# Two more products of the up projection in two levels, and the attention's last transposes divided

## The chip, the cores and the metric

The kernel runs on one core of one Trainium2 chip. The metric is the device time of the program in microseconds (us). A core has TensorE (PE, matrix products; its weight loads are listed as PEld), VectorE (DVE), ScalarE (ACT), GpSimd (POOL, here used to issue DMAs) and SyncE (SP, which issues DMAs too). PE reads SBUF and writes PSUM, whose banks are shared out by tags in this kernel.

## The reference

A lightning attention block over 4 batches, 8 heads, 768 tokens and head dimension 64, then a two-layer block on the 3072 x 512 result:

```python
for b in range(nb):                      # blocks of 64 tokens
    intra = np.einsum('bhic,bhjc->bhij', qb, kb) * Dmask[None]
    intra = np.einsum('bhij,bhjd->bhid', intra, vb)
    inter = np.einsum('bhid,bhde->bhie', qb * lam_pow[None], kv_state)
    out[:, :, sl] = intra + inter
    kv_state = lam_block[None, :, None, None] * kv_state + np.einsum('bhsd,bhse->bhde', kb_dec, vb)
x = attn_out.transpose(0, 2, 1, 3).reshape(B * S, H * D)     # 3072 x 512
h = x @ w_in                                                 # 512 -> 2048, "up"
g = h - np.tanh(h)
out = g @ w_out                                              # 2048 -> 512, "down"
```

All in float32.

## The kernel before, in words

**Groups.** Tokens are worked on in six groups of 512 (`NG = 6`, g = 0 to 5): 128 tokens of each of the four batches, a batch's part being a chunk. While group g goes through up and down, the attention of group g + 1 is done in between. The code from group 2 on (`GI = 2`) differs from that of the first two groups; the change concerns mostly groups 2 to 5.

**Products by seven.** Both projections use Strassen's scheme in Winograd's form: a 2 x 2 block product with seven products of blocks, P1 to P7, of sums of blocks, instead of eight. `FACT` names the two factors of each. In up, the four result blocks of the hidden layer are called 11, 12, 21 and 22, held as g11, g12, g21, g22 with a fifth tile, gS ("S1"); each is 128 x (4 u x 512): u counts four parts of the hidden dimension. The blocks come out as

- 11: P1 + P2
- 12: P1 + P6 + P5 + P3
- 21: P1 + P6 + P7 + P4
- 22: P1 + P6 + P7 + P5

**One or two levels.** An ordinary product of up for one u (`up(g, u, n)`) is four matmuls of 128x256, so sixteen for the four u. "In two levels" a product is itself done by the seven-product scheme, in seven steps of four matmuls of 128x128 (`STEPS = (1, 2, 6, 5, 7, 3, 4)`). For up that is `inner_steps`: before, for P1, P2 and P5 (`INNER`) of groups 2 to 5. Its weights for steps 5, 6, 3 are sums of weight quarters, made once by `inner_weights` in group 1, written to DRAM (`fine_in`) and read back a piece at a time; its token sums are made by `inner_tokens`. After the steps the results are put together by three DVE adds and four ACT copies of 128x512. For down, `down_twice` does the same, with hidden sums made by `sums_twice`; inside it, at its second step, DVE forms a12 - s2 (L817), which a later step (3) reads.

**Seeds.** A product that adds to a sum held in SBUF starts from a PSUM bank into which ACT has copied that sum (`seed`). Before, in groups 2 to 5, P6 is added to P1 in PSUM (bank "y" seeded with g12 by `seed_up`), copied back to g12 (L570), P7 and then P4 go on in the same bank, and P3 in a bank "z" seeded with P5 (g22). `finish` takes tanh (ACT, L561) and subtracts (DVE, L562).

**Order.** The last loop of the kernel, over g, writes out the order. Around the change, in groups 2 to 5: for each u the products P3, P7, P6 (of u + 2), P4, with the seven steps of down's P1 (`p_first`) spread among them; then down's P2, the first half of the attention's output of g + 1 (`att_out(g + 1, (0, 1))`), down's P4, P5, P6, the second half, P7; then P3 of down interleaved with P1 and P2 of up of the next group, then P5 of up and the first two P6. DVE also transposes the queries and keys of group g + 1 (`att_transpose`, L362 and L373, one chunk at a time) and decays its keys (`att_decay`, L399): chunks 0 and 1 in the loop over u, chunks 2 and 3 by `run(p1[0:1])` between down's P4 and P5. The weights of down and of `inner_steps` come through a ring of seven buffers (`RING`, `piece`, `send`) whose reads POOL issues in the order of `stream`, as buffers come free.

Instructions are put in their engine's queue by a scheduler that follows the written order unless something further down is ready sooner by its own estimate. `tied` (`keep_in_program_order`) pins an instruction behind the one written before it on the same engine.

Of the kernel before, what the change touches and what calls it, by code (L numbers as in the profile page):

```python
# [24 lines left out]
def kernel(  # L25
# [188 lines left out]
    TWICE = (3, 5, 6, 4, 7, 1, 2)  # L214
    fine = dram.tile([len(TWICE), len(SUB), 128, NU, 128], F32, name="fine")

    fine_in = dram.tile([3, 3, 128, NU, 128], F32, name="fine_in")
    w_in_u = moe_w_in.rearrange("k (a n) -> k a n", a=2)
    blocks = [("in", u, i) for u in range(NU) for i in range(KI)] + [("out", kt, a) for kt in range(KH)
                                                                    for a in range(2)]  # L220
# [180 lines left out]
    def kv_products(g, bs):  # L401

        kv = bank("kv", *(("yb", 1) if g >= GB else ("att", 4))).rearrange("d (b p e) -> d b p e", b=2, p=NP)
        for n, b in enumerate(bs):
            kd, vn = raw[g, b]["k"], raw[g, b]["v"]
            for p in range(NP):
                for j in range(2):
                    tied(g == 0, nc.tensor.matmul(out=kv[ts(j, 64), n, p, :], lhsT=kd[:, 2 * p + j, :],  # L408
                                                  rhs=vn[:, 2 * p + j, :], start=n == 0 and p == 0, stop=True,
                                                  skip_group_check=True))  # L410
        return kv
# [10 lines left out]
    def att_read(g, bs):  # L422
        ops = [bank("op", *x).rearrange("d (p b s) -> d p b s", p=2, b=2)
               for x in ((("ya", 1), ("z", 1)) if g >= GB else (("att", 4),) * 2)]
        decayed = None
        if g > 0:
            st = state[:, bs[0]:bs[0] + 2]
            for n, b in enumerate(bs):
                for p in (0, 1):
                    for j in range(2):  # L430
                        r = ts(j, 64)
                        for pp in (p, p + 2):
                            nc.tensor.matmul(out=out_dst(ops, n, pp, j), lhsT=state[r, b, pp, :],  # L433
                                             rhs=tr[g, b][2][r, pp, :], start=n == 0 and p == 0, stop=False,
                                             skip_group_check=True)
# [90 lines left out]
    def seed(key, x, tag, src):  # L526

        banks[key, x] = bank(x, tag, 1)
        tied(x == "y" and key[2] < 2, nc.scalar.activation(banks[key, x].rearrange("q (m c) -> q m c", m=2), src, AF.Copy))

    def hidden(g, c):

# [2 lines left out]
        return hid[g, c]  # L535

    def seed_up(g, u):
        seed(("up", g, u), "y", ("yb", "w", "ya")[u % 3], hidden(g, 12)[:, u])

    def up(g, u, n):  # L540
        a, bname = FACT[n]
        wt = {"A11": w1[u][:, 0:2, 0], "A12": w1[u][:, 2:4, 0], "S3": w1[u][:, 0:2, 1], "A22": w1[u][:, 2:4, 1],
              "S1": ws[u][:, 0], "S2": ws[u][:, 1], "S4": ws[u][:, 2]}[a]
        x = xt[g][bname] if bname != "B11" else xt[g, 0][:, 0:2]
        key = ("up", g, u)
        if g >= GI and n == 6 and u > 1:
            seed_up(g, u)
        if g >= GI and n == 3:
            seed(key, "z", "z", hidden(g, 22)[:, u])
        t, first = product_bank(key, n)  # L550
        for m in range(2):
            for kt in range(2):
                nc.tensor.matmul(out=t[:, m, :], lhsT=wt[:, kt, ts(m, 128)], rhs=x[:, kt, :],  # L553
                                 start=first and m == 0 and kt == 0, stop=kt == 1, skip_group_check=True)

        def dst(c):
            return hidden(g, c)[:, u]

        def finish(c, src):
            th = work.tile([128, 2, HB], F32, name="th", tag="th")  # L560
            nc.scalar.activation(th, src, AF.Tanh)  # L561
            nc.vector.tensor_tensor(dst(c), src, th, op=AL.subtract)  # L562

        y, z, w = (banks[key, x].rearrange("q (m c) -> q m c", m=2) if (key, x) in banks else None for x in "yzw")
        if n == 1:
            seed(key, "w", "w", y)
        elif n == 2:
            finish(11, w)
        elif n == 6:
            nc.scalar.activation(dst(12), y, AF.Copy)  # L570
        elif n == 7:
            if g < GI:
                nc.scalar.activation(dst(22), y, AF.Copy)
            nc.vector.tensor_tensor(dst(22), dst(22), z if g < GI else y, op=AL.add)  # L574
            finish(22, dst(22))
        elif n == 4:
            finish(21, y)
        elif n == 3:
            nc.vector.tensor_tensor(dst(12), dst(12), z, op=AL.add)  # L579
            finish(12, dst(12))  # L580
        if n == (3 if g < GI else 7):
            nc.vector.tensor_tensor(dst("S1"), dst(12), dst(22), op=AL.add)
            nc.vector.tensor_tensor(dst(12), dst(11), dst(12), op=AL.subtract)

# [7 lines left out]

    INNER = (1, 2, 5)
    toks = {}

    def a_quarter(n, u, i, k):
        return (ws[u][:, 0, k] if n == 5 else w1[u][:, 2 * n - 2 + k, 0])[:, ts(i, 128)]

    def inner_weights(u, ns=INNER):
        for n in ns:
            a11, a12, a21, a22 = (a_quarter(n, u, i, k) for i in range(2) for k in range(2))
            t = late["pool"].tile([128, 4, 128], F32, name="ws2", tag="sums", bufs=6)
            s1, s2, s4 = (t[:, x] for x in range(3))
            for dst, x, y, op in ((s1, a21, a22, AL.add), (s2, s1, a11, AL.subtract), (a21, a11, a21, AL.subtract),
                                  (s4, a12, s2, AL.subtract)):
                tc.keep_in_program_order(nc.vector.tensor_tensor(dst, x, y, op=op))
            (nc.sync if u == NU - 1 else nc.gpsimd).dma_start(out=fine_in[INNER.index(n)].rearrange("x p u c -> p u x c")[:, u], in_=t[:, 0:3])

    def inner_tokens(g):
        for n in INNER:
# [9 lines left out]

    def inner_steps(g, n):

        tags = {1: ("yb", "att", "att"), 2: ("w", "att", "att"), 5: ("ya", "att", "z")}[n]
        y, w, z = (bank(x, tag, 4 if tag == "att" else 1) for x, tag in zip(("y3", "w3", "z3"), tags))
        r5 = otile("r5")
        out4 = hidden(g, {1: 12, 2: 11, 5: 22}[n])
        c11, c12, c21, c22 = (out4[:, :, i, ts(j, 128)] for i in range(2) for j in range(2))
        for x in STEPS:  # L630
            b = toks[g, n][x]
# [30 lines left out]
    def pieces_of(g):  # L662
# [5 lines left out]
        for x in STEPS:  # L668
            yield g, 3, x
            if x in (3, 5, 6):  # L670
                yield from ((g + 1, ("in", n), x) for n in (1, 2))
        yield from ((g + 1, ("in", 5), x) for x in STEPS if x in (3, 5, 6))

    stream = [x for g in range(1, NG) for x in pieces_of(g)]
    sent = {"n": 0}
# [168 lines left out]
    def every(steps):  # L844
        for _ in steps:
            pass
# [181 lines left out]
    for g in range(1, NG):  # L1028
        last = g == NG - 1
        p0, p1 = attention(g + 1) if not last else ([], [])  # L1030
        if g < GI:
            p_first = down(g, 1)
        else:
            sums_twice(g, 1)
            p_first = down_twice(g, 1)
        for u in range(NU):
            if g < GI:
                for n in (2, 6, 5, 7, 1, 4, 3):
# [10 lines left out]
                            fine_pieces(*p)  # L1049
            else:  # L1050
                up(g, u, 3)
                up(g, u, 7)
                if u + 2 < NU:
                    up(g, u + 2, 6)
                else:
                    next(p_first)
                up(g, u, 4)
                if u + 1 == NU:
                    sums_twice(g, 2)
                if u != 2:  # L1060
                    steps(p_first, (2, 1, 0, 2)[u])
                if not last and u < 2:
                    att_transpose(g + 1, (u,))
                elif not last:
# [27 lines left out]
        if g == GI - 1:  # L1092
            inner_weights(NU - 1, INNER[:2])
            steps(p4, 4)
            inner_weights(NU - 1, INNER[2:])
# [44 lines left out]

# [28 lines left out]
```

## Time and profile before

| What | Value |
|---|---|
| Time, median of 3 runs | 653.97 us (653.42 to 654.21) |
| The profiled execution's own time | 652.32 us |
| Its span on the core | 650.5 us |
| Mean granted TensorE clock | 1.000 |
| PE busy | 641.9 us, 99% of the span |
| DVE busy | 499.6 us, 77% |
| ACT busy | 250.4 us, 38% |
| POOL busy | 242.1 us, 37% |
| DMA | 135.79 MB, mean 209 GB/s |

A trace row gives start and length in us, the engine, the line, the operation, the tile written and those read, the shape, the number of instructions merged into the row, and in brackets the engine's idle time before it with what ended it. Lengths include the pipeline's latency, so the distance from one start to the next is what an instruction occupies. Times are from the span's start.

### The profile page before, as it was taken

How to read it: one execution, taken by the hardware profiler on the slowest of the kernel's cores; microseconds unless marked ns; L12 is line 12 of the kernel's file. 1: busy time of each engine (PE TensorE's matmuls, PEld its weight loads, DVE VectorE, ACT ScalarE, POOL GpSimd, SP SyncE). 2: the span in 40 equal slices, each digit the busy share in tenths (PEclk: the TensorE clock that was granted, in tenths of full speed). 3: DMA queues.
4: the chain of work that ended last, by engine and by line, in shares of the span. 5: the costliest groups of instructions: out<-in, count | busy, mean ns of one | idle time of the engine just before them, and what ended most of it. 6: DMA issues, size and time to landing. Idle time of an engine off the chain costs nothing. (4 is left out here: it accounts for less than half of the span.)

```text
span 650.5 us, 15718 instructions
## 1 busy us (share of the span) xinstructions
PE 641.9 (99%) x6080; PEld 595.6 (92%) x6080; DVE 499.6 (77%) x969; ACT 250.4 (38%) x513; POOL 242.1 (37%) x418
## 2 busy tenths in 40 slices
PE   8999999999999999999999999999999999999998
PEld 7888888888888999999999989999998999998997
DVE  4467889968999895778986678998477997485873
ACT  3686765523222222533222453213453313264210
POOL 6000136767756335203335302443411354411341
PEclk9999999999999999999999999999999999999999
DMA  9869987988979758958757967766967686612474
GB/s 200 213 170 192 251 257 226 383 250 232 270 195 269 240 190 259 209 125 219 241 166 229 249 132 170 223 234 208 232 137 157 206 265 213 235 69 66 158 246 163
DMA packets 160281, 135.79 MB, mean 209 GB/s; under 512 B 128640, under 2 KB 130944, under 8 KB 160208
## 3 DMA queue, kind: packets, MB, share of 16 engines
q0 software_dynamic: 30496, 97.88, 47.0%
q1 hardware_dynamic: 128096, 36.53, 26.7%
q8 instruction: 48, 0.79, 0.5%
q10 hardware_dynamic: 1616, 0.39, 0.4%
q14 instruction: 25, 0.20, 0.1%
HBM read 110.10 MB, written 24.64 MB: 207 GB/s over the span
## 5 line engine op out<-in xcount | busy, mean ns | idle before, releaser
L696 POOL DMA_DIRECT2D wb<-fine x204 | 110.0, 540 | 245.7 <-PE y L811 159.6
L815 ACT ACTIVATE q<-y 128x128 f32<-128x128 f32 x112 | 31.0, 277 | 144.6 <-PE y L811 143.6
L811 PE MATMUL y<-wb,g 128*128 128x128 f32 x584 | 76.6, 277 | 0.0
L811 PEld LDWEIGHTS y<-wb,g 128*128 128x128 f32 x584 | 70.7, 192 | 0.7
L870 PE MATMUL h<-xt,w 128*128 128x256 f32 x256 | 57.8, 383 | 0.4 <-DVE w L325 0.4
L870 PEld LDWEIGHTS h<-xt,w 128*128 128x128 f32 x256 | 47.6, 190 | 7.9 <-DVE w L325 1.3
L811 PE MATMUL zw<-wb,g 128*128 128x128 f32 x368 | 48.7, 276 | 0.0
L561 ACT ACTIVATE th<-g 128x512 f32<-128x512 f32 x40 | 25.2, 630 | 60.0 <-DVE g L579 42.2
L562 DVE TENSOR_TENSOR g<-g,th 128x512 f32<-128x512 f32 x40 | 27.7, 691 | 24.5 <-ACT th L561 24.4
L811 PEld LDWEIGHTS zw<-wb,g 128*128 128x128 f32 x368 | 44.8, 192 | 0.2 <-DVE g L817 0.2
L553 PE MATMUL y<-xt,w 128*128 128x256 f32 x192 | 45.0, 380 | 0.0
L553 PEld LDWEIGHTS y<-xt,w 128*128 128x128 f32 x192 | 36.5, 190 | 5.0 <-ACT g L570 0.2
L553 PE MATMUL z<-xt,ws 128*128 128x256 f32 x160 | 38.8, 381 | 0.1
L553 PE MATMUL y<-tt,w 128*128 128x256 f32 x160 | 38.3, 382 | 0.0
L811 PE MATMUL zw<-wb,s 128*128 128x128 f32 x280 | 37.9, 276 | 0.0
L553 PE MATMUL y<-tt,ws 128*128 128x256 f32 x160 | 37.8, 380 | 0.0
L811 PE MATMUL y<-wb,s 128*128 128x128 f32 x280 | 37.5, 277 | 0.0
L811 PEld LDWEIGHTS zw<-wb,s 128*128 128x128 f32 x280 | 35.2, 192 | 0.4
L811 PEld LDWEIGHTS y<-wb,s 128*128 128x128 f32 x280 | 34.7, 192 | 0.7
L553 PEld LDWEIGHTS y<-tt,w 128*128 128x128 f32 x160 | 29.9, 190 | 4.7 <-DVE g L574 0.5
L900 PE MATMUL acc<-wt,g 128*128 128x256 f32 x144 | 33.5, 382 | 0.4 <-DVE g L906 0.2
L553 PEld LDWEIGHTS y<-tt,ws 128*128 128x128 f32 x160 | 29.9, 191 | 3.6
(215 smaller groups left out, 1448.8 us busy)
## 6 DMA issues: line engine op xcount, KB each, us to landing
wb<-fine POOLq DMA_DIRECT2D x204, 256.0 KB, 3.7
wb<-fine_in POOLq DMA_DIRECT2D x36, 256.0 KB, 4.3
raw<-in_moe_w_out_dram SPq DMA_DIRECT2D x12, 512.0 KB, 5.6
rest<-fine POOLq DMA_DIRECT2D x20, 256.0 KB, 4.5
raw<-in_moe_w_in_dram SPq DMA_DIRECT2D x16, 256.0 KB, 6.4
fine<-f POOLq DMA_DIRECT2D x16, 256.0 KB, 4.6
q_blk<-in_q_dram SPq DMA_DIRECT2D x128, 32.0 KB, 3.3
k_blk<-in_k_dram SPq DMA_DIRECT2D x128, 32.0 KB, 3.3
```

The source lines that it names most:

```text
L553: nc.tensor.matmul(out=t[:, m, :], lhsT=wt[:, kt, ts(m, 128)], rhs=x[:, kt, :], start=first and m == 0 and kt == 0, stop=kt == 1, skip_gro ...
L561: nc.scalar.activation(th, src, AF.Tanh)
L562: nc.vector.tensor_tensor(dst(c), src, th, op=AL.subtract)
L696: nc.gpsimd.dma_start(out=t.rearrange("p m c -> p (m c)"), in_=fine[TWICE.index(n_), SUB.index(x_)].rearrange("p u c -> p (u c)"))
L811: tied(x == STEPS[-1], nc.tensor.matmul(out=dst, lhsT=a[:, u, :], rhs=wb[:, ts(u, 128)], start=x in (1, 2) and u == 0, stop=u == NU - 1, s ...
L815: nc.scalar.activation(keep, dst, AF.Copy)
L870: tied(u == 0, nc.tensor.matmul(out=hm[c][:, m, :], lhsT=w1[u][:, i, a, ts(m, 128)], rhs=xt[0, t][:, i, :], start=m == 0 and i == 0, stop= ...
L900: nc.tensor.matmul(out=acc[n][:, r, :], lhsT=a[:, ts(r, 128)], rhs=b, start=kt == 0 and r == 0, stop=kt == KH - 1, skip_group_check=True)
```

## The change

P6 and P7 of up are done by `inner_steps` too in groups 2 to 5, P6 alternating with P5, then P7. Their results (P6 in g21, P7 in gS) are added to P1 (g12) by DVE in SBUF: `second_sum` forms P1 + P6 in g12, `seed_up` forms P1 + P6 + P7 in g21 and seeds the banks of P3 (with P5) and of P4 (with g21). In the loop over u only P3 and P4 remain as ordinary products, and g22 is completed by adding g21 instead of a PSUM bank. The steps of down's P1 are spread anew, and its sums (`sums_twice(g, 1)`) are made after the first P4 instead of ahead of the loop. The weight sums of P6 and P7 are made in group 1 beside down's P3, in the free tile gS. Of the attention, chunk 2 is transposed ahead of down's P5 and chunk 3 after P5's second step, where both stood ahead of P5 (this holds for every g but the last). Two kinds of attention matmuls (L408, L433) are tied from group 2 on, one kind of seed (L529) is no longer tied.

```diff
-    fine_in = dram.tile([3, 3, 128, NU, 128], F32, name="fine_in")
+    fine_in = dram.tile([5, 3, 128, NU, 128], F32, name="fine_in")
...
-                    tied(g == 0, nc.tensor.matmul(out=kv[ts(j, 64), n, p, :], lhsT=kd[:, 2 * p + j, :],
+                    tied(g == 0 or g >= GB, nc.tensor.matmul(out=kv[ts(j, 64), n, p, :], lhsT=kd[:, 2 * p + j, :],
...
-                            nc.tensor.matmul(out=out_dst(ops, n, pp, j), lhsT=state[r, b, pp, :],
+                            tied(g >= GB, nc.tensor.matmul(out=out_dst(ops, n, pp, j), lhsT=state[r, b, pp, :],
...
-        tied(x == "y" and key[2] < 2, nc.scalar.activation(banks[key, x].rearrange("q (m c) -> q m c", m=2), src, AF.Copy))
+        tied(False, nc.scalar.activation(banks[key, x].rearrange("q (m c) -> q m c", m=2), src, AF.Copy))
...
     def seed_up(g, u):
-        seed(("up", g, u), "y", ("yb", "w", "ya")[u % 3], hidden(g, 12)[:, u])
+        seed(("up", g, u), "z", ("z", "ya")[u % 2], hidden(g, 22)[:, u])
+        nc.vector.tensor_tensor(hidden(g, 21)[:, u], hidden(g, 12)[:, u], hidden(g, "S1")[:, u], op=AL.add)
+        seed(("up", g, u), "y", ("yb", "w")[u % 2], hidden(g, 21)[:, u])
+
+    def second_sum(g, u):
+        nc.vector.tensor_tensor(hidden(g, 12)[:, u], hidden(g, 12)[:, u], hidden(g, 21)[:, u], op=AL.add)
...
-        if g >= GI and n == 6 and u > 1:
-            seed_up(g, u)
-        if g >= GI and n == 3:
-            seed(key, "z", "z", hidden(g, 22)[:, u])
...
         elif n == 7:
-            if g < GI:
-                nc.scalar.activation(dst(22), y, AF.Copy)
-            nc.vector.tensor_tensor(dst(22), dst(22), z if g < GI else y, op=AL.add)
+            nc.scalar.activation(dst(22), y, AF.Copy)
+            nc.vector.tensor_tensor(dst(22), dst(22), z, op=AL.add)
             finish(22, dst(22))
...
         elif n == 3:
+            if g >= GI:
+                nc.vector.tensor_tensor(dst(22), dst(22), dst(21), op=AL.add)
+                finish(22, dst(22))
             nc.vector.tensor_tensor(dst(12), dst(12), z, op=AL.add)
             finish(12, dst(12))
-        if n == (3 if g < GI else 7):
+        if n == 3:
             nc.vector.tensor_tensor(dst("S1"), dst(12), dst(22), op=AL.add)
             nc.vector.tensor_tensor(dst(12), dst(11), dst(12), op=AL.subtract)
...
-    INNER = (1, 2, 5)
+    INNER = (1, 2, 5, 6, 7)
...
-            t = late["pool"].tile([128, 4, 128], F32, name="ws2", tag="sums", bufs=6)
+            if n < 6:
+                t = late["pool"].tile([128, 4, 128], F32, name="ws2", tag="sums", bufs=6)
+            else:
+                t = hidden(GI - 1, "S1")[:, u].rearrange("p m c -> p (m c)").rearrange("p (x c) -> p x c", x=4)
...
-        tags = {1: ("yb", "att", "att"), 2: ("w", "att", "att"), 5: ("ya", "att", "z")}[n]
+        tags = {1: ("yb", "att", "att"), 2: ("w", "att", "att"), 5: ("ya", "att", "z"), 6: ("yb", "att", "att"),
+                7: ("w", "att", "att")}[n]
...
-        out4 = hidden(g, {1: 12, 2: 11, 5: 22}[n])
+        out4 = hidden(g, {1: 12, 2: 11, 5: 22, 6: 21, 7: "S1"}[n])
...
-        yield from ((g + 1, ("in", 5), x) for x in STEPS if x in (3, 5, 6))
+        yield from ((g + 1, ("in", n), x) for x in STEPS if x in (3, 5, 6) for n in (5, 6))
+        yield from ((g + 1, ("in", 7), x) for x in STEPS if x in (3, 5, 6))
...
-        if g < GI:
-            p_first = down(g, 1)
-        else:
-            sums_twice(g, 1)
-            p_first = down_twice(g, 1)
+        p_first = down(g, 1) if g < GI else down_twice(g, 1)
...
                 up(g, u, 3)
-                up(g, u, 7)
-                if u + 2 < NU:
-                    up(g, u + 2, 6)
-                else:
+                if u + 1 == NU:
                     next(p_first)
                 up(g, u, 4)
+                if u == 0:
+                    sums_twice(g, 1)
+                if u + 2 < NU:
+                    seed_up(g, u + 2)
                 if u + 1 == NU:
                     sums_twice(g, 2)
-                if u != 2:
-                    steps(p_first, (2, 1, 0, 2)[u])
+                steps(p_first, (0, 2, 2, 2)[u])
...
-        run(p1[0:1])
         p5 = down_twice(g, 5)
-        steps(p5, 3)
+        if not last:
+            att_transpose(g + 1, (2,))
+        steps(p5, 2)
+        if not last:
+            att_transpose(g + 1, (3,))
+        steps(p5, 1)
...
-        inner_tokens(g + 1)
+        inner_tokens(g + 1, INNER[:3])
         sums_twice(g, 3)
-        p3, pa, pb, pc = (down_twice(g, 3), *(inner_steps(g + 1, n) for n in INNER))
-        for _ in STEPS:
+        p3, pa, pb, pc, pd, pe = (down_twice(g, 3), *(inner_steps(g + 1, n) for n in INNER))
+        rest = [(u, (n,)) for n in INNER[3:] for u in range(NU)] if g == GI - 1 else []
+        for x in STEPS:
             next(p3)
             next(pa)
             next(pb)
+            if rest:
+                inner_weights(*rest.pop(0))
         for p in (pa, pb, p3):
             every(p)
+        for r in rest:
+            inner_weights(*r)
+        inner_tokens(g + 1, INNER[3:])
         for x in STEPS:
-            if x == STEPS[-1]:
-                up(g + 1, 0, 6)
             next(pc)
-            if x in (7, 3):
-                seed_up(g + 1, int(x == 3))
+            next(pd)
             if x in (1, 6, 7):
                 first_sum(g + 1, (1, 6, 7).index(x))
         every(pc)
+        every(pd)
         first_sum(g + 1, 3)
-        up(g + 1, 1, 6)
+        for u in range(NU):
+            next(pe)
+            second_sum(g + 1, u)
+        every(pe)
+        for u in (0, 1):
+            seed_up(g + 1, u)
```

More of the change, by code (lines that the diff above doesn't have):

```diff
@@ L432, in att_read @@
                         for pp in (p, p + 2):
-                            nc.tensor.matmul(out=out_dst(ops, n, pp, j), lhsT=state[r, b, pp, :],
-                                             rhs=tr[g, b][2][r, pp, :], start=n == 0 and p == 0, stop=False,
-                                             skip_group_check=True)
+                            tied(g >= GB, nc.tensor.matmul(out=out_dst(ops, n, pp, j), lhsT=state[r, b, pp, :],
+                                                           rhs=tr[g, b][2][r, pp, :], start=n == 0 and p == 0, stop=False,
+                                                           skip_group_check=True))
             for p in (3, 2, 1, 0):
@@ L591, in first_sum, with inner_weights @@
         nc.vector.tensor_tensor(c11, c11, th, op=AL.subtract)
-    INNER = (1, 2, 5)
+    INNER = (1, 2, 5, 6, 7)
     toks = {}
     def a_quarter(n, u, i, k):
-        return (ws[u][:, 0, k] if n == 5 else w1[u][:, 2 * n - 2 + k, 0])[:, ts(i, 128)]
-    def inner_weights(u, ns=INNER):
+        return (ws[u][:, n - 5, k] if n in (5, 6) else w1[u][:, k, 1] if n == 7 else w1[u][:, 2 * n - 2 + k, 0])[:, ts(i, 128)]
+    def inner_weights(u, ns=INNER[:3]):
         for n in ns:
             a11, a12, a21, a22 = (a_quarter(n, u, i, k) for i in range(2) for k in range(2))
-            t = late["pool"].tile([128, 4, 128], F32, name="ws2", tag="sums", bufs=6)
+            if n < 6:
+                t = late["pool"].tile([128, 4, 128], F32, name="ws2", tag="sums", bufs=6)
+            else:
+                t = hidden(GI - 1, "S1")[:, u].rearrange("p m c -> p (m c)").rearrange("p (x c) -> p x c", x=4)
             s1, s2, s4 = (t[:, x] for x in range(3))
@@ L609, in inner_weights, with inner_tokens @@
             (nc.sync if u == NU - 1 else nc.gpsimd).dma_start(out=fine_in[INNER.index(n)].rearrange("x p u c -> p u x c")[:, u], in_=t[:, 0:3])
-    def inner_tokens(g):
-        for n in INNER:
+    def inner_tokens(g, ns):
+        for n in ns:
             x = xt[g][FACT[n][1]]
@@ L1094 @@
             steps(p4, 4)
-            inner_weights(NU - 1, INNER[2:])
+            inner_weights(NU - 1, INNER[2:3])
         every(p4)
-        run(p1[0:1])
         p5 = down_twice(g, 5)
-        steps(p5, 3)
+        if not last:
[4 more added lines that the diff above has]
+        steps(p5, 1)
         sums_once(g, 21, 21, 11)
```

## The prediction

> **What bounds the kernel now.** I read the page's busy line first, then a table by stages (chosen from the timeline of group 4, the fifth of six), then PE's and DVE's timelines inside them.
>
> ```profile
> PE 641.9 (99%) x6080; PEld 595.6 (92%) x6080; DVE 499.6 (77%) x969; ACT 250.4 (38%) x513; POOL 242.1 (37%) x418
> ```
> ```profile
> 449.30:467.46 18.16, 18.16 (x165) 18.16 (x164) 9.61 (x17) 5.29 (x11) 9.16 (x17) 1.00 0.92 237
> 467.46:477.40 9.94, 9.94 (x75) 9.50 (x74) 8.22 (x14) 7.52 (x14) 2.07 (x4) 1.00 0.96 233
> 477.40:508.14 30.74, 30.74 (x169) 27.68 (x168) 22.91 (x37) 12.31 (x23) 5.24 (x10) 1.00 0.66 150
> 508.14:530.41 22.27, 21.92 (x314) 21.20 (x312) 21.89 (x40) 5.68 (x18) 11.09 (x22) 1.00 0.68 221
> ```
> Columns: length, then busy time of PE, PEld, DVE, ACT, POOL; granted clock, DMA share, GB/s. The stages are P3 of down beside up's P1 and P2 in two levels; P5 in two levels with the first of P6; the rest of up beside down's P1; down's P2, P4, P5 with attention. PE is busy throughout, so its work is the time as long as nobody is later than PE. DVE has room in the first stage (9.6 of 18.2 us), some in the third (22.9 of 30.7), none in the fourth.
>
> PE, group 4:
> ```profile
> 467.46 1.06 PE L637 MATMUL y<-tt,ws 128*128 128x128 f32 x8
> 468.35 1.06 PE L637 MATMUL w<-tt,ws 128*128 128x128 f32 x8
> 474.78 1.05 PE L637 MATMUL y<-tt,ws 128*128 128x128 f32 x8
> 475.67 1.89 PE L553 MATMUL y<-tt,ws 128*128 128x256 f32 x8
> 477.40 1.89 PE L553 MATMUL z<-xt,ws 128*128 128x256 f32 x8
> 484.30 1.06 PE L811 MATMUL y<-wb,g 128*128 128x128 f32 x8
> ...
> 529.00 1.06 PE L811 MATMUL y<-wb,gS 128*128 128x128 f32 x8
> 530.41 1.16 PE L811 MATMUL zw<-wb,gS 128*128 128x128 f32 x8 [0.35 <-DVE gS L817]
> ```
> The trace counts each matmul twice: x8 is four. Start to start, a step of a two-level product (four matmuls) takes 0.893 us (467.46 to 468.35), an ordinary product of one u 1.725 (477.40 to 484.30 is four). The last two lines are the one real wait: the second starts 1.41 after the first, 0.52 late, held by L817.
>
> DVE and ACT, group 4:
> ```profile
> 475.87 0.60 ACT L641 ACTIVATE g<-y 128x512 f32<-128x512 f32 x1
> 484.22 0.69 DVE L583 TENSOR_TENSOR g<-g,g 128x512 f32<-128x512 f32 x1
> 485.19 0.69 DVE L562 TENSOR_TENSOR g<-y,th 128x512 f32<-128x512 f32 x1 [0.28 <-ACT th L561]
> 485.80 0.70 DVE L362 STREAM_TRANSPOSE qt<-q_blk 128x512 f32<-128x512 f32 x1
> 486.43 0.67 DVE L362 STREAM_TRANSPOSE kt<-k_blk 128x512 f32<-128x512 f32 x1
> 487.02 0.65 DVE L373 TENSOR_TENSOR qd<-qt,fwd 128x512 f32<-128x512 f32 x1
> ...
> 511.03 0.68 DVE L794 TENSOR_TENSOR s<-g,s 128x512 f32<-128x512 f32 x1
> 511.63 0.68 DVE L794 TENSOR_TENSOR s<-g 128x512 f32<-128x512 f32 x1
> ```
> A 128x512 operation occupies DVE for 0.605 us (511.03 to 511.63), a chunk's two transposes and decay product 1.79 (485.80 to 487.02 and 0.57). The ACT copy ends at 476.47, 0.80 after PE left that step (475.67).
>
> **PE's work.** An ordinary product is 4 x 1.725 = 6.90 us over the four u, in two levels 7 x 0.893 = 6.25. Two products in groups 2 to 5: 8 x 0.65 = **-5.2 us**.
>
> **Transposes.** In groups 2 to 4 the transposes of chunks 2 and 3 stand ahead of L817 on DVE, and P5's sixth step waits for L817: 0.71, 0.69 and 0.52 us late by its starts (327.35, 429.32, 530.41), with 0.1 each to restart. Now L817 has only one chunk's 1.79 us ahead of it, comes 1.79 earlier, and the wait goes: **-2.2 us**. What is late next is L739, whose place in DVE's sum is unchanged. Group 1 had no such wait, the last group has no transposes. The moved call issues no DMA: its group is loaded as a whole much earlier.
>
> **DVE's work.** Per product and group three adds of 128x512 in the inner steps and four small sums of tokens; per u one add in second_sum and one in seed_up; the add into g22 stays, only with another operand. That is 14 x 0.605 + 8 x 0.2 (L618's spacing) = 10.1 us more per group. ACT gets eight copies and loses four: 2.4 us; it was at 12.3 of 30.7.
>
> What matters is where it lies. P5 and P6 alternate, then P7: 21 x 0.893 = 18.8 us of PE, beside which DVE has only adds, first_sum and second_sum (21 x 0.605 = 12.7 us) and idles the rest. All else in up needs P7, because g21 = P1+P6+P7 feeds both g22 and the seed of P4. So DVE's large share starts only when P7 ends. Count from there to what down's P2 needs, the last u's g21:
> - DVE: 4 adds of seed_up; 7 per u (28) less the last u's L582 and L583, which may follow; 4 of sums_twice(g,1): 34 x 0.605 = 20.6. Transposes of two chunks, 3.6. One decay (L399), 0.6. Sum 24.8; the first can start 0.83 after P7 (the ACT copy), so the last result is there at 25.7.
> - PE: 8 x 1.725 + 7 x 0.893 (down's P1) = 20.05, and three quarters of P2's first step, 0.67: it is there at 20.7.
>
> PE waits 5.0 us in groups 2 and 3, 4.4 in group 4 (its successor needs no decay), 0.8 in group 5 (no attention): **+15.2 us**. Before, the same count is about as much DVE work, but beside 30.7 us of PE. Nothing fills the wait: P2's second step needs bank w, held by the last u's g21; the attention's matmuls are tied behind P2; P4's weights take over P2's ring slots. From P2 on, DVE and PE follow each other as before (fourth row), so the wait is not recovered.
>
> **Costed at nothing.** The first P4 needs its seed (0.83 + 0.6 + 0.1 + 0.6 = 2.1 after P7, PE has 1.7 to do): 0.4, swallowed by the later wait, up to 1.6 in all without it. 24 more weight reads of 256 KB on POOL's queue, 0.54 of issue each: six in 12.5 us, where 13 in 18.2 us (first row, 237 GB/s) held nobody; if that cover fails, a read's 4.3 us to landing bounds it in each group. Weight sums of P6 and P7, once, 8 x 4 x 0.2 = 6.4 us of DVE in group 1, beside P3, where DVE idles 6.5 in one piece; at most some 2 us. The moved sums_twice(g,1) is counted above. The ties cost nothing where PE follows the written order; below nothing they cannot go, for they only forbid filling.
>
> **Sum.** -5.2 - 2.2 + 15.2 = +7.8. On the profiled execution's 652.32 us that is 660.1; the median of the runs is 1.65 above it, so I forecast **661.8**. Bounds: an operation that reads DVE's previous result starts 0.72 after it (the sums at 476.02 and 476.74), some ten per group: up to +4.8; L582 and L583 of the last u ahead of g21: another 1.2 in each group. Down: if u = 2's two also follow, -1.2 per group, and part of the handoffs at 0.6 may overlap better. Own range 656 to 668.
>
> **Rivals.**
> *DVE is not late: faster.* If L582, L583, transposes and decay all queue behind the g21 results, DVE needs 24.8 - 6 x 0.605 - 4.2 = 17.0 us and PE never waits. All of -7.4 remains: 646.5; with half of it deferred, about 651. It decides at 19.8 us of DVE work ahead of g21. For it: those L582 and L583 are free to move. Against: in the rows above L583 runs before g21's L562 though later users could wait, and the transposes come directly after; they are tied behind what is written before them.
>
> *The wait slows PE's clock.* The trace starts so: 16 records from 1.06 to 4.63 us, 0.22 each instead of 0.112, until 6.44. Afterwards the granted clock is 1.00, and no idle is over 1.1 us. Should a wait of 4 to 5 us bring that back, the next 5.4 us do half their work: 2.7 x 3 = 8.1 more, 669.9. [...]
> [...]
>
> *The weights come late.* The second row's DMA share of 0.96 leaves little for six more reads: 1.5 MB at 233 GB/s are 6.5 us, up to 4 x 6.5 less what up's 0.66 has free; 665 to 675. Against: no wait of PE for wb in any row.
>
> *The transposes land ahead of L817 after all:* 2.2 less gained, 664.0, within the range.
>
> **Chances.** Forecast 0.52, clock 0.14, weights 0.05: slower 0.71. DVE not late, whole 0.14, half 0.10: faster 0.24. In between 0.05. The border of 0.2% is 1.3 us, about what a measurement of this kernel can tell from no change. The range 649 to 671 leaves out the whole-gain case and some 0.06 above.
>
> **What the profile after would show.** PE: after P7's last step eight products (L553) and seven steps, then one idle of 4 to 5 us at P2's first or second step, released by DVE's L562, in groups 2, 3, 4, under 1 us in group 5. DVE without idle from P7's end to there, about 25 us. No idle at "zw<-wb,gS". PE busy down by 5, span up. Wrong if DVE shows idle in that stretch, if g21's L562 of the last u stands well ahead of L582, or if PE's wait is elsewhere (wb, a seed). Granted clock below 1.0 after the wait decides the second rival.

## The result, and the profile after

The changed kernel takes 714.33 us (median of 6 runs, 711.13 to 717.52) where the kernel before took 653.62 in the same comparison: the ratio is 1.0936, 95% interval 1.0907 to 1.0964. The prediction was 661.8 us, at most 671. Its sign was right and its size was not: about 37 us come from a step that it had costed at nothing, and the time without them, 677.09, would still be above 671.

PE's start of each group's interleaved P3 / P1 / P2 stage (the first matmul of `inner_steps` in a group: L645, before L637) cuts the trace into groups. Lengths in us, from the profiled execution of each kernel; the experiments named here follow below:

| kernel | first such start | group 2 | group 3 | group 4 | group 5 and end |
|---|---|---|---|---|---|
| before | 245.4 | 102.2 | 102.0 | 100.5 | 100.3 |
| after | 247.8 | 149.4 | 109.0 | 108.3 | 99.7 |
| sums on POOL's queue | 246.9 | 110.2 | 109.5 | 107.5 | 100.9 |
| products in the wait | 246.5 | 109.0 | 107.2 | 105.0 | 100.0 |
| six sums left out | 249.1 | 105.3 | 105.1 | 101.4 | 99.3 |
| transposes only | 247.6 | 101.8 | 101.4 | 100.0 | 100.3 |
| P6 and P7, early sums | 246.0 | 110.4 | 103.2 | 101.2 | 99.6 |

(A group begins with its own first products of up, which lie beside down's P3 of the group before it. The start-up ahead of the first column differs by 1 to 4 us from run to run and is left out of the comparisons by group.) Two things stand out: one loss of some 40 us that occurs once, in group 2, and one of 7 to 8 us in each of groups 2, 3 and 4, not in group 5.

From the page of the kernel after: the busy line, the granted clock in 40 slices, and three rows of the costliest groups (busy time, mean ns of one, idle time ahead and what ended it):

```profile
PE 650.5 (91%) x6272; PEld 607.0 (85%) x6272; DVE 540.3 (76%) x1089; ACT 258.0 (36%) x529; POOL 259.9 (36%) x448
...
PEclk9999999999999997569899999899999989999999
...
L820 PE MATMUL y<-wb,g 128*128 128x128 f32 x584 | 79.7, 280 | 16.1 <-DVE g L564 15.7
L702 POOL DMA_DIRECT2D wb<-fine_in x60 | 32.4, 541 | 75.7 <-DMA fine_in<-gS 38.9
...
L645 PE MATMUL y<-tt,wb 128*128 128x128 f32 x160 | 21.3, 285 | 36.0 <-DMA wb<-fine_in 36.0
```

PE was busy for 99% of the span and is now busy for 91%. Two rows of idle time carry it: 36.0 us in which the inner step of a two-level product waits for its weights (`fine_in`, the DRAM copy of the weight sums), and 15.7 us in which down's P2 waits for g21 (L564). The clock row shows a deep dent in the middle and three shallow ones. Before, it was:

```profile
PEclk9999999999999999999999999999999999999999
```

**Where the 36 us arise.** Around 300 us, in group 1's last stage: SP's queue, POOL, DVE and PE (start, length, engine, line, operation, and the idle time just before with what ended it).

```profile
254.91 11.42 SPq L171 DMA_DIRECT2D q_blk<-in_q_dram  x16
...
299.89 1.85 SPq L159 DMA_DIRECT2D v_nat<-in_v_dram  x3
301.83 3.77 SPq L616 DMA_DIRECT2D fine_in<-gS  x2
```
```profile
304.73 2.69 POOL L702 DMA_DIRECT2D wb<-fine_in  x5 [37.03 <-DMA fine_in<-gS]
```
```profile
256.32 0.28 DVE L615 TENSOR_TENSOR gS<-ws,gS 128x128 f32<-128x128 f32 x1
...
304.18 0.29 DVE L615 TENSOR_TENSOR gS<-w 128x128 f32<-128x128 f32 x1 [30.68 <-DMA fine_in<-gS]
```
```profile
271.06 1.11 PE L645 MATMUL y<-tt,ws 128*128 128x128 f32 x8
308.19 2.07 PE L645 MATMUL y<-tt,wb 128*128 128x128 f32 x8 [36.02 <-DMA wb<-fine_in]
311.42 1.83 PE L645 MATMUL z<-tt,wb 128*128 128x128 f32 x7 [1.16 <-DMA wb<-fine_in]
```

`inner_weights` sends the sums of u = 3 to DRAM on SP's queue (L616: `nc.sync if u == NU - 1`). The sums of P6 for u = 3 are ready when DVE ends the row of 256.32, at 256.60. But from 254.91 SP issues the attention loads of group 3, 82 of them by the rows (64 of blocks, 18 of natural layout), until 301.8: some 0.57 us each. The write is issued behind them at 301.83, 45 us after its sums, and P7's behind it. POOL reads the sums back from 304.73, and PE starts at 308.19, 36.2 us late. DVE stands too, 30.68 us by its row, for P7's sums reuse a tile that P6's write must leave first. The kernel before writes the sums of P1, P2 and P5 by the same line of code, but earlier. SP's queue of the kernel before:

```profile
216.13 1.73 SPq L609 DMA_DIRECT2D fine_in<-ws  x3
252.48 6.94 SPq L171 DMA_DIRECT2D q_blk<-in_q_dram  x13
```

There the writes are issued 36 us ahead of the loads.

**Where the 7 to 8 us per group arise.** Group 4 by stages (length, busy time of PE, PEld, DVE, ACT, POOL, then clock, DMA share, GB/s). The stages: P3 beside P1 and P2; P5, P6, P7 in two levels; P3 and P4 beside down's P1; the last step of down's P1 and P2 up to its second step; the rest with attention.

```profile
506.19:524.06 17.87, 17.87 (x163) 17.87 (x161) 10.84 (x24) 5.29 (x11) 8.86 (x17) 1.00 0.94 245
524.06:543.67 19.61, 19.61 (x172) 19.29 (x171) 13.42 (x21) 10.06 (x18) 5.29 (x10) 1.00 0.90 222
543.67:562.79 19.12, 19.12 (x113) 17.18 (x111) 18.29 (x31) 8.86 (x18) 4.82 (x9) 1.00 0.72 170
562.79:570.18 7.39, 2.57 (x18) 2.19 (x17) 7.39 (x14) 3.04 (x6) 1.07 (x2) 0.89 0.50 175
570.18:592.00 21.82, 21.67 (x289) 20.95 (x289) 18.84 (x34) 4.76 (x15) 8.62 (x16) 0.88 0.47 146
```

DVE has 6 us of room beside P5 to P7, under 1 us in the third stage, none in the fourth, and there PE works 2.57 us of 7.39. PE and DVE at that place, group 4:

```profile
542.68 1.16 PE L645 MATMUL y<-tt,w 128*128 128x128 f32 x8
...
562.79 1.50 PE L820 MATMUL y<-wb,g 128*128 128x128 f32 x12
566.26 0.49 PE L820 MATMUL y<-wb,g 128*128 128x128 f32 x2 [1.97 <-DVE g L564]
569.60 0.80 PE L820 MATMUL y<-wb,g 128*128 128x128 f32 x2 [2.85 <-DVE g L564]
570.18 1.92 PE L820 MATMUL zw<-wb,g 128*128 128x128 f32 x8
```
```profile
544.50 1.29 DVE L540 TENSOR_TENSOR g<-g,gS 128x512 f32<-128x512 f32 x2 [1.06 <-ACT gS L649]
...
567.92 0.41 DVE L833 TENSOR_TENSOR q<-q,zw 128x256 f32<-128x256 f32 x1
568.25 0.69 DVE L586 TENSOR_TENSOR gS<-g,g 128x512 f32<-128x512 f32 x1
568.86 0.68 DVE L564 TENSOR_TENSOR g<-y,th 128x512 f32<-128x512 f32 x1
```

P2's first step needs g21 of one u after another; the third u's comes 2.13 late by start-to-start times, the fourth's another 3.01. In groups 2 and 3 it is 2.13 and 3.62; in group 5 the fourth u's is 0.29 late and the third's not. DVE runs without a gap from 544.50 to 569.54. The last matmul row above shows the second effect: its four matmuls take 1.71 from start to start (the next row starts at 571.89), where 0.89 is normal. The granted clock is 0.5 from 568.59 to 575.41, and likewise for 6.83 us after the wait in groups 2 and 3.

### The profile page after: what moved, and what is told of

The parts are those of the page before. It is cut to its first block, busy times and chain, and to the rows that moved or that the text cites. A ratio compares the mean times of both kernels' runs of the same rounds, so it can differ in the third digit from the quotient of the medians.

```text
span 714.2 us, 16327 instructions
## 1 busy us (share of the span) xinstructions
PE 650.5 (91%) x6272; PEld 607.0 (85%) x6272; DVE 540.3 (76%) x1089; ACT 258.0 (36%) x529; POOL 259.9 (36%) x448
## 4 chain that ended last, share of the span: by engine, by line
PE 56%; DVE 14%; DMA 12%; issue 8%; SPq 7%; POOL 2%; ACT 1%; DVEq 0%; POOLq 0%
PE y L820 11%; PE zw L820 9%; PE h L879 7%; SPq L171 5%; PE acc L909 4%; PE y L555 4%; DMA q_blk<-in_q_dram 3%; PE y L645 3%; DMA k_blk<-in_k_dram 3%; SPq L159 2%; DVE g L564 2%; PE z L645 2%; PE z L555 2%; PE op L462 2%; PE sp L387 2%
## 5 line engine op out<-in xcount | busy, mean ns | idle before, releaser
L820 PE MATMUL y<-wb,g 128*128 128x128 f32 x584 | 79.7, 280 | 16.1 <-DVE g L564 15.7
L702 POOL DMA_DIRECT2D wb<-fine_in x60 | 32.4, 541 | 75.7 <-DMA fine_in<-gS 38.9
L645 PE MATMUL y<-tt,wb 128*128 128x128 f32 x160 | 21.3, 285 | 36.0 <-DMA wb<-fine_in 36.0
L820 PE MATMUL zw<-wb,g 128*128 128x128 f32 x368 | 51.5, 285 | 1.0 <-DVE g L826 0.6
L645 PEld LDWEIGHTS y<-tt,wb 128*128 128x128 f32 x160 | 19.7, 199 | 36.6 <-DMA wb<-fine_in 36.2
L820 PEld LDWEIGHTS zw<-wb,g 128*128 128x128 f32 x368 | 47.3, 201 | 1.4 <-DVE g L826 0.8
L820 PE MATMUL y<-wb,s 128*128 128x128 f32 x280 | 39.8, 289 | 0.0
L649 ACT ACTIVATE g<-y 128x512 f32<-128x512 f32 x48 | 28.6, 595 | 31.2 <-PE y L645 31.2
L820 PEld LDWEIGHTS y<-wb,s 128*128 128x128 f32 x280 | 37.1, 204 | 0.7
L656 DVE TENSOR_TENSOR g<-r,y 128x512 f32<-128x512 f32 x16 | 11.0, 688 | 31.4 <-PE y L645 22.4
```

What stands on the lines that cost most here:

```text
L645: nc.tensor.matmul(out=dst[:, ts(u, 128)], lhsT=a, rhs=b, start=x in (1, 2, 5) and u == 0, stop=True, skip_group_check=True)
L649: op = tied(n == 5, nc.scalar.activation({1: c11, 4: c21, 6: c12}[x], d, AF.Copy))
L702: nc.gpsimd.dma_start(out=t.rearrange("p m c -> p (m c)"), in_=fine_in[INNER.index(n_[1]), (5, 6, 3).index(x_)].rearrange("p u c -> p (u c)"))
L820: tied(x == STEPS[-1], nc.tensor.matmul(out=dst, lhsT=a[:, u, :], rhs=wb[:, ts(u, 128)], start=x in (1, 2) and u == 0, stop=u == NU - 1, s ...
```

## The experiments

**Only the write's queue.** The changed kernel with the sums of P6 and P7 sent by POOL's queue for every u.

```diff
-            (nc.sync if u == NU - 1 else nc.gpsimd).dma_start(out=fine_in[...
+            (nc.sync if u == NU - 1 and n < 6 else nc.gpsimd).dma_start(out=fine_in[...
```

> The changed kernel with one edit: the last u's weight sums of P6 and P7 are written to DRAM from POOL's queue instead of SP's. Theory A (SP's queue): after the change that write stands behind 76 attention loads on SP, is issued at 301.8 us, the reads of it hold POOL's queue for 37 us and PE for 36, and PE then runs at half clock to 316, 4 us more. With the write issued some 2 us after its sums, all of this goes: 40 to 42 us off, 672 to 675 us, and what remains over the kernel before is the waits at down's P2 with their half-clock stretches. Rival B (the reads are late because the DMA engines are shared with the attention loads, or the tile gS is held): PE still waits over 10 us at P6's third step, and the time stays above 685.

Measured: 677.09 us (675.76 to 677.52), ratio to before 1.0362 (1.0339 to 1.0385). One queue name is worth 37 us of medians (714.33 to 677.09, a little less than the 40 to 42 expected), 39 of the profiled spans, and the table puts all of it into group 2 (149.4 to 110.2). P6's last sums now leave at 257.30, and PE no longer waits for P6's weights. A wait of 1.3 is left at 280.45, at the first step of P7 that reads weight sums. POOL's reads of them:

```profile
276.29 1.64 POOL L702 DMA_DIRECT2D wb<-fine_in  x3 [5.61 <-PE z L645]
```

The last write of P7's sums lands at 275.62 in this trace, and the read that PE waits for is issued at 276.84 and lands at 280.32. So rival B, a cause other than SP's queue, is out for the 36 us. The waits at P2 stay as they were. PE in group 3 of this kernel:

```profile
413.67 1.50 PE L820 MATMUL y<-wb,g 128*128 128x128 f32 x12
417.13 0.49 PE L820 MATMUL y<-wb,g 128*128 128x128 f32 x2 [1.96 <-DVE g L564]
421.07 0.80 PE L820 MATMUL y<-wb,g 128*128 128x128 f32 x2 [3.45 <-DVE g L564]
421.66 1.92 PE L820 MATMUL zw<-wb,g 128*128 128x128 f32 x8
...
426.80 1.13 PE L820 MATMUL y<-wb,s 128*128 128x128 f32 x8
427.77 1.06 PE L820 MATMUL zw<-wb,s 128*128 128x128 f32 x8
```

After the wait the steps of P2 take 1.72 us until 426.95, where the clock is granted in full again, then 0.89 to 0.97. So the 677 that remain are the change without its accident, and they are still 24 above before.

**Only the divided transposes.** The kernel before with that one edit.

```diff
-        run(p1[0:1])
         p5 = down_twice(g, 5)
-        steps(p5, 3)
+        if not last:
+            att_transpose(g + 1, (2,))
+        steps(p5, 2)
+        if not last:
+            att_transpose(g + 1, (3,))
+        steps(p5, 1)
```

> The kernel before with only the transposes of chunks 2 and 3 divided by P5's second step. Theory: the waits of 0.5 to 0.7 us before zw<-wb,gS in groups 2 to 4 go and nothing takes their place: 2.2 us off, ratio 0.9966. Rival: chunk 3's transposes, now behind L817, push the sums that P5's end and P6 read, and PE waits there by as much: 653.6, ratio 1.000.

Measured: 652.27 us (10 runs), ratio 0.9983 (0.9969 to 0.9997). The wait that the prediction showed at L811, 0.52 late in group 4, is gone, and PE's steps now follow at 0.89:

```profile
530.22 1.06 PE L811 MATMUL y<-wb,gS 128*128 128x128 f32 x8
531.11 1.06 PE L811 MATMUL zw<-wb,gS 128*128 128x128 f32 x8
532.01 1.06 PE L811 MATMUL y<-wb,gS 128*128 128x128 f32 x8
```

Groups 2, 3 and 4 are 0.4 to 0.6 shorter, 1.5 in all. Group 1, where nothing waited before, loses 0.7 at an attention product (L462, at 214.5). By medians 1.0 is left of the 2.2 forecast.

**Fewer operations on DVE.** The kernel with POOL's queue, without six of the eight 128x512 operations that form S1 and g11 - g12 in each of groups 2 to 5: the sums of the first three u are left out of the computation.

```diff
-        if n == 3:
+        if n == 3 and (g < GI or u == NU - 1):
```

> As e1, but in groups 2 to 5 gS = g12 + g22 and g12 = g11 - g12 are left out for the first three u (six DVE operations of 128x512 per group, 3.6 us, all ahead of the last g21 on DVE); what reads them takes what lies there. Theory C (DVE's amount of work sets the wait at down's P2): the wait of 5.7 us in groups 2 and 3 falls to about 2.1, in group 4 to 1.5, too short to halve the clock, so each of the three groups also wins the 2.3 us lost at half clock: 17 to 18 us under e1, 655 us. Rival D (PE waits there for a bank or a weight read, whatever DVE has to do): the wait stays over 5 us and the time within 2 us of e1's.

Measured: 661.13 us, ratio 1.0121 (1.0088 to 1.0155), 16 below the kernel with POOL's queue where 17 to 18 were expected. The wait at P2 becomes one of 2.45 in groups 2 and 3 and 1.25 in group 4, instead of 5.74 and 5.14: 3.3 to 3.9 less for six operations of 0.6. That is DVE's count as such, and rival D, a bank or a weight read, is out. Most of the rest is the clock; in group 2 a new wait of 1.2 at an attention product (L462, at 321.84) takes some of the gain back. Four windows of this kernel (columns as above), the first two in group 3, the others in group 2:

```profile
411.98:415.39 3.41, 1.12 (x10) 0.93 (x9) 3.41 (x7) 0.92 (x4) 1.07 (x2) 1.00 1.05 303
415.39:418.80 3.41, 3.41 (x18) 3.41 (x17) 3.41 (x7) 0.16 (x1) 1.18 (x3) 0.50 0.90 272
306.17:309.58 3.41, 1.89 (x17) 1.69 (x16) 3.41 (x7) 1.64 (x4) 2.15 (x4) 1.00 0.97 282
309.58:313.00 3.42, 2.66 (x22) 2.65 (x23) 3.42 (x8) 0.28 (x1) 1.08 (x3) 1.00 1.11 308
```

The same wait of 2.45 us halves the clock in group 3 and does not in group 2. That the waits left over would be too short to halve it was the author's estimate; the one in group 3 did. Changes of the granted clock in these runs fall on a grid of 3.41 us: in the changed kernel they stand at 275.04, 316.00, 350.13, 356.96 and 459.36, which is 12, 10, 2 and 30 times 3.413 apart (184.32 us in 54 steps). In group 3 the wait lies inside one window of that grid, PE works 1.12 us of it, and the next window is granted half. In group 2 it straddles two, with 1.89 and 2.66 us of work, and nothing follows. (The start-up of this execution has one window at half clock as well, at 19.44, which the comparison by groups leaves out.)

**Work in the wait.** The kernel with POOL's queue, with 22 spare matmuls (128x128, into a bank that nobody reads) ahead of P2 in groups 2 to 4.

```diff
+            if not last:
+                spare = bank("spare", "att", 4)
+                for _ in range(22):
+                    tied(True, nc.tensor.matmul(out=spare[:, 0:128], lhsT=fwd[:, 0, :], rhs=fwd[:, 0, :], start=True, stop=True))
```

> As e1, but in groups 2 to 4 PE does 22 spare matmuls of 128x128 (4.9 us, into a free bank, used by nobody) just ahead of down's P2, where it otherwise waits 5.4 to 6.0 us for DVE. Theory E (a wait of that length halves the clock for two windows): with PE busy the granted clock stays 1.00, the remaining wait is about 1 us, and the half-speed work after it (some 2.3 us per group) is won: 6 to 8 us under e1, 669 to 671. Rival F (the time is DVE's alone, PE's slow stretch is hidden because DVE stays behind): the clock stays 1.00 but the time is e1's, 676 to 678.

Measured: 670.61 us (669.48 to 671.41), ratio 1.0272 (1.0241 to 1.0303): work that serves nothing makes the kernel 6.5 us faster by medians (5.9 when each is compared with the kernel before in its own comparison), as theory E expected. PE in group 3 and the clock row of the page:

```profile
412.99 5.08 PE L1090 MATMUL spare<-fwd 128*128 128x128 f32 x44
417.90 0.83 PE L820 MATMUL y<-wb,g 128*128 128x128 f32 x6
419.50 0.49 PE L820 MATMUL y<-wb,g 128*128 128x128 f32 x2 [0.77 <-DVE g L564]
419.83 1.06 PE L820 MATMUL zw<-wb,g 128*128 128x128 f32 x8
```
```profile
PEclk9999999999999999999999999999999999999999
```

The step after the wait takes 0.89. DVE is hardly sooner: from the start of down's last P1 step and P2's first (412.10, just ahead of the rows shown; 413.67 without the spare work) to P2's second step it takes 7.7 us, against 8.0. What was idle is filled, little more. Without the spare work PE runs at half speed from the end of the wait (421.07) to 426.95, which costs half of that, 2.9 us. Groups 3 and 4 get 2.3 and 2.5 of it back; in group 3 a wait of 0.51 appears at 448.44, which is not in the kernel without the spare work. Group 2 gets 1.2, because its wait for P7's weights (280.96) is 2.2 here instead of 1.3. Another 0.9 comes in group 5, which has no spare work; why is not shown.

**P6 alone in two levels,** P7 an ordinary product as before, first with the sums of P1 where before has them, then with them made early, beside P6's steps (the core of the edit against the kernel with POOL's queue).

```diff
-    INNER = (1, 2, 5, 6, 7)
+    INNER = (1, 2, 5, 6)
...
+                up(g, u, 7)
```

> Only P6 is done in two levels besides P1, P2, P5; P7 stays an ordinary product added to P1 + P6 in PSUM; the last u's write goes from POOL's queue; transposes divided; two steps of down's P1 stand ahead of the loop over u. Theory C: PE saves 4 x 0.65 = 2.6 us and the 2.2 of the transposes. DVE ahead of the last g21 has 30 x 0.605 + 4.2 = 22.4 us beside 27.6 of PE, so no wait at P2: 649 us, ratio 0.993. Rival: second_sum and the seeds at the end of P5 and P6 are a chain of 2 us that two steps of P1 do not cover, and DVE's extra seven adds make PE wait there: 1 to 2 us in each of four groups, 653 to 657.

The second kernel against the first:

```diff
-            sums_twice(g, 1)
...
+            if x == 7:
+                sums_twice(g + 1, 1)
```

> As w6, but sums_twice(g,1) is made beside P5 and P6, where DVE idles, instead of ahead of the loop over u, with first_sum one step earlier; the read of the state (L433) is tied only from group 3 on. Theory C: 2.4 us of DVE less between P6's end and the last g21, so the waits at P2 (1.6 us in groups 2 and 3) and at the first seeds (0.6) go, as do 0.5 us in group 1: 2.6 us of PE and 1 us of the transposes remain, 649.5 us, ratio 0.994. Rival: the early sums delay second_sum and the seeds behind it, PE waits there, and the time is w6's or worse, 656 to 658.

Measured: 658.07 (ratio 1.0070, 1.0047 to 1.0093) and 655.07 (12 runs, 1.0034, 1.0015 to 1.0053). Both stay above before, where 649 and 649.5 were expected. (In the second kernel L433 is also tied from group 3 on only.) In groups 2 and 3 the first kernel waits 0.73 and 0.65 at P2's first two steps, the second 0.66 and 0.65: the early sums took nothing from that place. In group 2 DVE, freed of four sums (2.4 us), stands some 2.3 us waiting for ACT's tanh (L562) instead, and from 299.75 on it goes without a gap through other operations (among them L583, L399, L584 and P1's finishing adds) that stand ahead of the last g21 in both kernels. Their groups 2 and 3 take 103.0 to 104.0, against 101.4 to 101.8 with the transposes alone. Group 5 gains: 100.0 and 99.7 against 100.3.

**P6 and P7 in two levels, with DVE's work spread:** the kernel with POOL's queue, with the sums of down's P1 made beside P5 and P6, one chunk's transposes of the next group beside P7, L433 tied from group 3 on only, and S1 and g11 - g12 of the last two u made after g21.

```diff
-        if n == 3:
+        if n == 3 and (g < GI or u < 2):
...
+                    late_sums(g, 2)
+                    late_sums(g, 3)
...
+            if x == 7:
+                sums_twice(g + 1, 1)
...
+        if g + 2 < NG:
+            att_transpose(g + 2, (0,))
```

> As e1 with three moves of DVE work: sums_twice(g,1) beside P5 and P6, chunk 0's transposes beside P7, and gS and g11 - g12 of the last two u behind sums_twice(g,2); L433 tied only from group 3 on. Theory C: DVE has 24.8 - 2.4 - 1.8 - 1.2 = 19.4 us ahead of the last g21, and 0.8 to start, beside 20.7 of PE: the waits of 5.4 to 6 us fall under 1, the clock stays 1.00, PE's 5.2 us and 1 us of the transposes are won; the four deferred operations cost at most 2 us later in each of groups 2 to 4: 647 to 653 us, ratio 0.990 to 0.999. Rival: DVE has no room anywhere between P7's end and P3, so what is taken from ahead of P2 is waited for at P4 and P5: 3 us or more in each of three groups, 656 or more.

Measured: 659.81 us (655.44 to 663.66), ratio 1.0101 (1.0063 to 1.0139), where the theory gave 647 to 653 and its rival 656 or more. The waits at P2 shrink from 5.74 to 1.20 in groups 2 and 3 and to 0.60 in group 4. New ones of about 0.8 per group appear at L462 for DVE's `ss`, and once, before group 2's P3 and P4, PE waits 3.0 for P7's weights:

```profile
278.68 1.06 PE L649 MATMUL w<-xt,w 128*128 128x128 f32 x8
282.61 0.77 PE L649 MATMUL z<-tt,wb 128*128 128x128 f32 x2 [2.87 <-DMA wb<-fine_in]
```

POOL issues the write and the reads of P7's sums no later than in the kernel with POOL's queue (268.28 and 276.16, against 268.42 and 276.29), but the read that PE waits for takes 5.8 us to land instead of 3.5. Why it takes longer is not shown. This wait halves the clock for 6.83 us as well. Groups 3 and 4 take 103.2 and 101.2, longer than before by 1.2 and 0.7; only group 5 keeps a gain, 0.7.

**P6 in two levels where DVE has most room,** groups 4 and 5, with the divided transposes; two kernels that differ in which attention matmuls and seeds are held to the written order.

```diff
+    G6 = 4
...
-        yield from ((g + 1, ("in", 5), x) for x in STEPS if x in (3, 5, 6))
+        yield from ((g + 1, ("in", n), x) for x in STEPS if x in (3, 5, 6) for n in ((5, 6) if g + 1 >= G6 else (5,)))
...
+        rest = [(u, (6,)) for u in range(NU)] if g == G6 - 1 else []
```

> The divided transposes, and up's P6 in two levels in groups 4 and 5 only (P7 stays one product with its own seed-and-sum path; the weights of P6 are summed beside down's P3 of group 3 and written by POOL's queue). Theory (what the change gives is PE's saving, wherever VectorE still has room, and the only groups with room are the last two, whose chunks carry less attention): P6 alone for groups 2 to 5 gave 655.07, of which groups 2 and 3 waited 1.8 us each at down's P2, while group 5 took 99.7 us instead of 100.4. So 652.3 of the transposes alone, less 0.7 in group 5 and 0 to 0.7 in group 4: about 651.2, ratio 0.996 to 0.998, with waits at down's P2 under 0.5 us in group 4 and none in group 5. Rival (VectorE has no room anywhere: what PE saves is waited for in group 4 as in groups 2 and 3): 652.3 plus 1.2, about 653.5, ratio 1.000 or above.

> The same as the kernel beside it, with attention's matmuls into shared banks kept in written order in the late groups and the seeds of up's first two steps no longer kept so, as in the change. Theory: the order of these few instructions moves the time by under 1 us, so 650.5 to 652.5. Rival: the written order holds PE back where it stood free before, as once in group 1 of the changed kernel (0.5 us), and three more times here: 1 to 2 us above the kernel beside it.

Measured: 651.76 us, ratio 0.9981 (0.9965 to 0.9998), and 652.32, 0.9984 (0.9968 to 0.9999). Neither can be told from the transposes alone (0.9983). By groups the first takes 100.6 and 99.8, against 100.0 and 100.3: group 5 gains 0.5, where 0.7 was expected, and group 4 loses 0.6. Group 4 has no wait at P2, but PE's rows show several small delays that the kernel with the transposes alone does not have there: 0.47 for a late weight read at 535.95, 0.25 for a seed at 500.36, 0.3 at an attention product (L473, at 518.14), and some 0.4 where attention matmuls (L433, at 510.58) stand between steps of P2. Their sum, 1.4, is about the 0.6 lost and the 0.65 that PE should save. The ties made no measurable difference.

## Why the prediction was wrong

**"Costed at nothing", the weight sums of P6 and P7: this step failed.** It counted DVE's 6.4 us, "at most some 2 us", and not the DMAs that the same call issues. One of four writes goes to SP's queue. For P1, P2 and P5 it is issued ahead of the attention loads, but for P6 and P7 it stands behind 82 of them. It was worth 37 us, more than all other terms together: the wait for P6's weights that it led to is the "wb" that the prediction named as a sign of being wrong. The rows for it stood in the trace of before: SP's loads from 252.48, and the earlier write at 216.13.

**DVE's work: right in mechanism, place and groups, mis-sized in one count.** Waits at P2 in groups 2, 3, 4, next to none in group 5, released by the g21 result of L564, were forecast at 5.0, 5.0, 4.4 and 0.8 and came at 5.75, 5.75, 5.14 and 0.29, each of the first three in two pieces: 16.9 instead of 15.2. In group 4 the first add starts 0.93 after P7's end and the last g21 ends 25.0 later; the forecast was 0.83 and 24.2. Most of the difference, 0.9 in all, is read from the rows: the last u's S1 (L586, 0.6) and a down operation (L833, 0.33) stand ahead of the last L564. The prediction let the last u's two sums follow, and had them ahead of g21 only in its bounds, at up to 1.2.

**The clock: the rival came true in addition to the forecast.** The forecast left PE's clock at full speed after waits of 4 to 5 us. It gave the other case a chance of 0.14 and priced it at 8.1 us, an estimate from the 5.4 us at half speed with which the trace of before starts. In the kernel with POOL's queue the half clock costs some 2.9 us in each of groups 2 to 4, 8.7 in all, and spare work in the waits took 6.5 off the time. The half clock is also why PE's busy time rose by 8.6 us (641.9 to 650.5) where the prediction had it fall by 5: in the changed kernel PE was busy for 22.1 us at half clock, so by estimate 11 us less at full clock, which would leave a fall of some 2.5. The changes of the clock in these runs lie on a grid of 3.41 us, and a wait of 2.45 us was enough where it lay in one window of that grid, with 1.12 us of work.

**Transposes:** the waits went, as forecast, but 0.4 to 0.6 per group came of it and group 1 lost 0.7: -1.0 instead of -2.2.

**PE's work:** the steps keep their 0.893 us, so 0.65 per product are saved, 1.3 per group. In group 5, where DVE has room, the kernels with both products and nothing left out take 99.6 to 100.9 against 100.3: of 1.3, at most 0.7 arrives. A late weight read takes the rest where it occurs (0.43 and 0.79 in the kernel with POOL's queue). So the rival of late weights was small there. The one large wait for weights had another cause than the DMA share that this rival named: SP's queue.

**By groups** the kernel with POOL's queue adds up to within 0.8 us. In group 3: -1.3 for PE, -0.5 for the transposes, +5.75 for the wait, +2.9 for the half clock is +6.9; measured 109.5 - 102.0 = 7.5. In group 4: -1.3 - 0.5 + 5.14 + 2.9 = 6.2; measured 7.0. In group 2, with 1.3 for the late read of P7's weights, 8.2; measured 8.0.

**The rival "DVE is not late"** fell: DVE runs without a gap up to the last g21, and the wait shrank by 3.3 to 3.9 us when six operations were left out. Where DVE's work was spread instead, the waits at P2 fell to 1.20 and 0.60, but new ones of about 0.8 per group came at L462. No version with P6 or P7 in two levels was shown to be faster than the transposes alone.

## What to carry to other kernels

When a step is moved, list every DMA that it issues and read, for each queue, what will stand ahead of it at the new place; a small write behind 82 prefetches was here as late as the last of them, 45 us after its sums. Saved matmul time was lost again here, 1.3 us per group against waits of 5.75, 5.75 and 5.14, because the adds that replace it landed on an engine with no room before the next consumer; so count that engine's operations between the last input and the first use, in the order in which they are really queued. Price a wait of PE with its length and with half of the time at half clock that follows it: by estimate from the windows above, 1.7 us after the 2.45 us wait and 2.9 us after the waits of 5.7 us.

## What the runs showed that was not expected

- In these runs the granted clock changed on a grid of 3.41 us. A 2.45 us wait halved it for one window where PE worked 1.12 us of the window, and not where the same wait left 1.89 and 2.66 us of work in two. Over the runs, windows at full clock with 0.49, 1.12 and 1.34 us of work (POOL's queue at 416.71, six sums left out at 411.98, early sums at 278.40) were followed by half clock, and windows with 1.83, 1.87 and 1.89 us (products in the wait at 279.38, POOL's queue at 413.30, six sums left out at 306.17) were not. Waits of 5.7 us, broken by 0.33 us of work, halved it for two windows, 6.83 us, the second of which was granted half although PE had been back at work for most of the first.
- 22 matmuls whose result nobody reads, put into a wait, made the whole kernel 6.5 us faster (677.09 to 670.61 by medians).
- One write on SP's queue, behind 82 loads issued at some 0.57 us each, held PE for 36 us while POOL stood for 37.03 us waiting to read it back.
